# Attention with beacons and an ELU feed-forward layer: w_in in eight wide transfers, v halves by even and odd columns, and a new order of all steps

## The chip, the cores and the metric

The kernel runs on one core of one Trainium2 chip. The metric is the device time of one execution in microseconds (us). Three executions of the kernel before the change took 333.45, 333.01 and 333.42 us, with a median of 333.42 us.

## The reference: what is computed

Eight batches of eight heads, 576 tokens, 64 columns a head, and 16 beacon keys ahead of each head's own keys. The beacons are seen by every query, the own keys causally. The result, laid out as 4608 tokens of 512 numbers, goes through a feed-forward layer.

```python
k_all = np.concatenate([beacon_k, k], axis=2)
v_all = np.concatenate([beacon_v, v], axis=2)
scores = scale * np.matmul(q, k_all.transpose(0, 1, 3, 2))
...
a = np.exp(scores)
a /= a.sum(-1, keepdims=True) + 1e-09
...
x = np.ascontiguousarray(attn_out.transpose(0, 2, 1, 3)).reshape(B * S, H * D)
h = x @ w_in
g = np.where(h > 0.0, h, alpha * (np.exp(np.minimum(h, 0.0)) - 1.0))
return (g @ w_out).astype(np.float32)
```

w_in has 512 rows and 2048 columns, w_out 2048 rows and 512 columns, and the output is 4608 by 512 in float32.

## The kernel before, in words

**Order.** Nothing here is scheduled by a compiler. The program is a list of some 1,550 short words in `run("""...""")`; each word calls one small function ("step") that puts its instructions on their engines. So each engine works through its own instructions in the order of the words, and waits for what they need. A word is a step's letter and its numbers: F.0.1 is the step F for token tile 0, unit 1. Words that matter here:

- lq, lv, wi, wo: the loads, issued on POOL. lq.b.n.h0.h1 loads q and k of batch b (line 136), lv.b.j a piece of 128 keys (the first also holds the 16 beacons, the last has 80) of v (lines 147 and 152), wi a piece of w_in (line 161), wo.i a quarter of w_out (line 165). lk.b.i copies q or k of the batches 3 to 7 into a scratch in DRAM in a type of half the size (line 795), and lt.b.i brings them back transposed by two transfers on SP (line 802). lt.b.0 brings q's and lt.b.1 k's.
- T, ck, cq: transposes of q and k on PE (line 276) for the batches 0 to 2, drained by ACT or DVE (line 289). S is a score matmul (line 330), x its exponential on ACT (line 345), m a causal mask on DVE (line 350).
- L, n: the row sums on PE (line 390, with a column of ones) and their reciprocals on ACT (lines 451 and 454). W is attention times v on PE (line 390 too: one helper, quad, serves both), and M scales it into x, which is stored as xT, features by tokens, on DVE (lines 488, 498, 505). For batch 0 these steps come in two pieces, A (queries 0 to 255) and B (256 to 575), so that the first token tile can begin early.
- F: x times w_in on PE (line 528); e and u: the exponential and the positive part on ACT (lines 538 and 543); k, or r and g: the ELU put together on DVE (lines 553, 560, 566).
- G, o, s: g times w_out for the token tiles 0 and 1, its copy out of PSUM by DVE into a buffer osb (line 582), and the store by SP (line 588). From tile 2 on, w_out is multiplied by a Strassen scheme in seven products: Q on PE (line 650), wt and Z for the sums of its operands (line 596), J for the sums of its results, which for four of the seven end in a buffer osb and a store by SP (lines 671 and 674). From tile 4 on, w_in is partly done so too (H, X, P, K, E, U, V).
- warm, wm, wh: matmuls of zeros that keep PE at work early (lines 206, 214, 223).

**Buffers.** osb has three buffers, shared by o and J: a step that fills one waits until an earlier store from it has landed. A store is queued on SP behind whatever the list puts ahead of it there, the transposing transfers of lt among them. v has two buffers (batches in turn). POOL's loads use eight semaphores in turn, so that a load also waits until the one eight places ahead of it has landed.

**Features.** x's 512 features lie in four chunks of 128 partitions. Four heads share a pair of chunks, each on 32 partitions: the first 32 of a head's 64 columns go to one chunk, the others to the other. Line 390's matmul takes such 32 columns of v as its stationary operand, and w_in's rows are loaded to fit: 32 partitions and two chunks at a time.

Of the kernel before, what the change touches and what calls it, by code (L numbers as in the profile page):

```python
# [12 lines left out]
ALU = mybir.AluOpType  # L13
# [4 lines left out]
def kernel(  # L18
# [240 lines left out]
    @step  # L259
    def wi(c, n):  # L260
        load_wi(c, n)
# [119 lines left out]
    def quad(b, g, qa, qe, t, half, first):  # L381


        v16 = None if half is None else vt[b]
        pcs = [(j, max(a, qa), min(e, qe), c + max(a, qa) - a) for (j, a, e, c) in lays[b]
               if max(a, qa) < min(e, qe)]
        for n, (j, a, e, c) in enumerate(pcs):
            for i in range(4):
                h, p = 4 * g + i, 2 * g + i // 2
                nc.tensor.matmul(  # L390
                    out=t[32 * i:32 * (i + 1), a - qa:e - qa],
                    lhsT=ones[0:kc[j], :] if half is None else v16[0:kc[j], j, h, 32 * half:32 * (half + 1)],
                    rhs=et(b, p)[0:kc[j], i % 2, c:c + e - a],
                    start=(first and n == 0), stop=(n == len(pcs) - 1), skip_group_check=True)
# [206 lines left out]
    def wt(n, h_):  # L601
# [3 lines left out]
        elif n == 2:  # L605
            sub(T2[:, c], B22[:, c], T1[:, c])
        elif n == 3:
            sub(B12[:, c], B22[:, c], B12[:, c])
        else:
            sub(T4[:, c], B21[:, c], T2[:, c])  # L610

    @step
    def Z(t, n, h_, eng="v"):
# [4 lines left out]
        elif n == 1:  # L618
            sub(A(t, h_, 0, 1), A(t, h_, 0, 1), A(t, h_, 1, 1), ALU.add, eng)
        elif n == 2:  # L620
            sub(A(t, h_, 0, 0), A(t, h_, 0, 1), A(t, h_, 0, 0), eng=eng)
        else:
            sub(A(t, h_, 1, 0), A(t, h_, 1, 0), A(t, h_, 0, 0), eng=eng)
# [194 lines left out]
    def run(names):  # L818
        for word in names.split():
            f, *args = word.split(".")  # L820
            op[f](*[a if a in "ABRpvs" else int(a) for a in args])
# [3 lines left out]
    lq.0.0.0.4 warm.12 lq.0.1.0.4 ident bt bk cb.0.3 wm.2 T.0.0.0 T.0.1.0 ck.0.1.0 cb.0.1 cb.0.0  # L825
    cq.0.0.0 cb.0.2 wm.6 S.0.0.0 x.0.0.0 S.0.1.0 x.0.1.0 T.0.0.1 T.0.1.1 ck.0.1.1 cq.0.0.1 wm.6
    S.0.0.3 S.0.0.1 cb.1.0 x.0.0.3 lq.0.0.4.8 T.0.2.0 cq.0.2.0 T.0.3.0 x.0.0.1 S.0.1.2 x.0.1.2 wm.5
    S.0.1.1 x.0.1.1 wm.5 S.0.1.3 x.0.1.3 tri m.0.0.3 m.0.0.0 lq.0.1.4.8 T.0.2.1 cq.0.3.0 S.0.0.2
    x.0.0.2 wm.5 S.0.3.0 T.0.3.1 x.0.3.0 cq.0.2.1 lq.1.0.0.4 S.0.2.0 x.0.2.0 wm.5 S.0.2.1 x.0.2.1
    lv.0.0 lv.0.1 wm.5 S.0.2.3 x.0.2.3 wi.0.0 wi.0.7 lv.0.2 wm.4 T.1.1.0 ck.1.1.0 T.1.0.0 m.0.2.0  # L830
    m.0.1.0 m.0.3.0 L.0.A n.0.A m.0.1.2 m.0.0.2 cq.0.3.1 S.0.3.1 x.0.3.1 cq.1.0.0 W.0.A.0 M.0.A.0
    S.0.3.3 S.0.2.2 x.0.3.3 x.0.2.2 W.0.A.1 m.0.2.3 m.0.3.3 m.0.1.3 M.0.A.1 wh.3 S.0.3.2 wh.5 S.1.2
    x.0.3.2 x.1.2 wh.4 S.1.5 wi.0.5 wi.0.1 x.1.5 wi.0.3 wi.0.6 wi.0.2 wi.0.4 F.0.1 e.0.1 cb.1.1
    S.1.3 x.1.3 F.0.0 u.0.0 e.0.0 lv.0.4 wi.1.0 m.0.3.2 r.0.1 cb.1.2 m.0.2.2 L.0.B lv.0.3 wi.1.3
    W.0.B.0 n.0.B M.0.B.0 g.0.1 S.1.4 F.0.2 x.1.4 S.1.1 e.0.2 x.1.1 k.0.0 W.0.B.1 M.0.B.1 lq.1.0.4.8
    T.1.2.0 ck.1.2.0 r.0.2 g.0.2 F.1.1 u.1.1 e.1.1 T.1.3.0 cq.1.3.0 S.1.6 wi.1.1 cb.1.3 x.1.6 wi.1.7
    wi.1.6 wi.1.5 wi.1.2 wi.1.4 F.0.4 S.1.0 m.1.0.1 wo.0 e.0.4 r.0.4 g.0.4 x.1.0 F.1.7 e.1.7 k.1.1
    r.1.7 g.1.7 S.1.12 x.1.12 S.1.7 cb.2.2 G.0.0.0 x.1.7 F.0.5 e.0.5 r.0.5 S.1.9 x.1.9 g.0.5 F.0.7
    e.0.7 r.0.7 S.1.10 x.1.10 S.1.11 x.1.11 G.0.1.0 F.0.3 g.0.7 m.1.0.0 D.1.0.0 u.0.3 S.1.8 x.1.8
    e.0.3 m.1.1.0 D.1.1.0 k.0.3 F.1.6 u.1.6 cb.2.1 e.1.6 lq.2.0.0.8 T.2.3.0 ck.2.3.0 T.2.2.0  # L840
# [134 lines left out]
```

## Time and profile before

| | us |
|---|---|
| median of three runs | 333.42 |
| the profiled execution itself | 332.93 |
| its span, from first to last instruction | 331.2 |
| PE busy | 321.2 |
| DVE busy | 300.4 |
| ACT busy | 291.8 |
| POOL busy | 100.7 |
| mean granted TensorE clock, share of full speed | 0.994 |

The engines are PE (TensorE matmul), PEld (its weight loads), DVE (VectorE), ACT (ScalarE), POOL (GpSimd) and SP (SyncE). A row of a timeline holds the start, the time taken, engine, line, operation, result<-operands, the shape and the count; behind it, in brackets, stands the idle time of the engine ahead of the row and what ended it. The waits view holds engine, tile and line, what was waited for, and then the total in us, the number of times and the longest. A row of windows holds the stretch, its length, and the busy time (with instructions) of PE, PEld, DVE, ACT and POOL, then the granted clock, the mean busy share of the transfers in flight and GB/s. SPq is SP's own queue. Of a transfer, the row gives the time that its issue takes on the engine; when it lands is told by the line "DMA to landing".

### The profile page before, as it was taken

What the parts mean: (1) busy time and instruction counts of PE and PEld (TensorE: products, weight loads), DVE (VectorE), ACT (ScalarE), POOL (GpSimd) and SP (SyncE); (2) the same over time, 40 slices, a digit from 0 to 9 for tenths busy, and PEclk for the clock granted to TensorE, in tenths of its full rate; (3) what the DMA queues carried; (4) which work ended last, traced back from release to release, by engine and by line L of the source; (5) the groups of instructions that cost most, each with busy time, mean ns of one, the idle gap of its engine ahead of it and who ended that gap; (6) DMA issues with size and microseconds to landing.
All of it is one profiled execution on the core that took longest, in us unless ns stands there. A gap on an engine that the chain in (4) does not pass through costs nothing.

```text
span 331.2 us, 8770 instructions
## 1 busy us (share of the span) xinstructions
PE 321.2 (97%) x3572; PEld 213.8 (65%) x3572; DVE 300.4 (91%) x568; ACT 291.8 (88%) x481; POOL 100.7 (30%) x121
## 2 busy tenths in 40 slices
PE   8989999999999979999999999999999999999995
PEld 3545666544445546765676566756766888888884
DVE  3573999999999799999999999999999999999981
ACT  1989999799999979999999999999988778889941
POOL 8866745583049218900120348000000000000000
PEclk9998999999999999999999999999999999999999
DMA  9999999999989959999591995610111011020113
GB/s 115 141 165 186 204 196 174 163 154 175 65 90 133 147 138 87 193 170 165 75 148 53 119 71 109 91 35 2 63 36 34 0 65 64 2 97 33 34 65 127
DMA packets 129080, 34.65 MB, mean 105 GB/s; under 512 B 112912, under 2 KB 127504, under 8 KB 129040
## 3 DMA queue, kind: packets, MB, share of 16 engines
q0 software_dynamic: 94912, 18.49, 67.5%
q1 hardware_dynamic: 33552, 15.47, 21.3%
q8 instruction: 28, 0.46, 0.6%
q10 hardware_dynamic: 576, 0.13, 0.2%
q14 instruction: 12, 0.10, 0.1%
HBM read 37.22 MB, written 15.34 MB: 159 GB/s over the span
## 4 chain that ended last, share of the span: by engine, by line
PE 78%; DVE 7%; DMA 5%; ACT 4%; POOL 4%; SPq 1%; issue 1%; DVEq 0%; ACTq 0%; POOLq 0%
PE ops L650 25%; PE hps L528 20%; PE hps L732 11%; PE sc L330 6%; PE ut L390 5%; PE ops L575 4%; DMA v<-in_v_dram 3%; DMA out_dram<-osb 2%; PE ut L650 2%; DVE gt L553 1%; SPq L802 1%; DVE qk L410 1%; PE lt L436 1%; POOL qst L136 1%; POOL kst L136 1%
## 5 line engine op out<-in xcount | busy, mean ns | idle before, releaser
L345 ACT ACTIVATE et<-sc 128x1024 f16<-128x1024 f32 (+2 forms) x114 | 105.3, 988 | 3.3 <-PE sc L330 2.9
L528 PE MATMUL hps<-xT,w_in 128*128 128x512 f16 (+1 forms) x448 | 95.4, 350 | 1.7 <-ACT r L543 1.5
L650 PEld LDWEIGHTS <-gt 128*128 128x128 f16 x768 | 74.1, 98 | 16.3 <-issue 2.7
L528 PEld LDWEIGHTS <-w_in 128*128 128x128 f16 x448 | 40.9, 98 | 36.7 <-issue 6.2
L538 ACT ACTIVATE e<-hps 128x512 f32<-128x512 f32 x96 | 59.0, 626 | 3.2 <-DVE gt L553 2.0
L553 DVE SCALAR_TENSOR_TENSOR gt<-e,r 128x512 f16<-128x512 f32 x84 | 56.5, 681 | 0.0
L543 ACT ACTIVATE r<-hps 128x512 f16<-128x512 f32 x84 | 51.5, 622 | 3.1 <-PE hps L528 2.6
L147 POOL DMA_DIRECT2D v<-in_v_dram x40 | 44.1, 1192 | 26.4 <-PE ut L390 13.5
L650 PE MATMUL ops<-w_out,gt 128*128 128x256 f16 x368 | 48.4, 273 | 0.0
L650 PE MATMUL ops<-wt,gt 128*128 128x256 f16 x352 | 46.3, 273 | 0.2 <-DVE osb L671 0.2
L596 DVE TENSOR_TENSOR gt<-gt 128x1024 f16<-128x1024 f16 x48 | 32.3, 681 | 0.1
L771 DVE SCALAR_TENSOR_TENSOR gt<-e,r 128x512 f16<-128x512 f32 x48 | 31.8, 681 | 0.1
L350 DVE TENSOR_TENSOR et<-et,triu 128x1024 f16<-128x1024 f16 (+4 forms) x66 | 26.8, 447 | 2.5 <-ACT et L345 2.4
L742 ACT COPY kst<-hps 128x512 f32<-128x512 f32 x36 | 21.3, 594 | 5.6 <-PE hps L732 5.3
L390 PEld LDWEIGHTS <-v 128*32 128x32 f16 (+1 forms) x800 | 17.6, 96 | 12.0 <-issue 2.6
L390 PE MATMUL ut<-et,v 128*32 128x464 f16 (+3 forms) x560 | 21.1, 296 | 0.4 <-ACT et L345 0.4
L732 PEld LDWEIGHTS <-w_in 128*128 128x128 f16 x192 | 18.6, 98 | 2.9
L671 DVE TENSOR_TENSOR osb<-ops,sm 128x512 f32<-128x512 f32 x23 | 15.6, 683 | 3.6 <-DMA out_dram<-osb 2.3
L810 POOL MEMSET qst<- 128x96 bf16 x5 | 0.9, 178 | 55.8 <-PE sc L330 53.3
L410 DVE TENSOR_TENSOR qk<-qk,et 128x1344 f16<-128x1344 f16 (+2 forms) x30 | 17.5, 582 | 0.2
L488 DVE TENSOR_TENSOR xT<-ut,rl 128x672 f16<-128x672 f32 (+12 forms) x26 | 16.4, 668 | 0.2
L575 PE MATMUL ops<-w_out,gt 128*128 128x512 f16 x64 | 16.2, 381 | 0.0
(126 smaller groups left out, 524.6 us busy)
## 6 DMA issues: line engine op xcount, KB each, us to landing
out_dram<-osb SPq DMA_DIRECT2D x35, 256.0 KB, 2.3
v<-in_v_dram POOLq DMA_DIRECT2D x24, 128.0 KB, 8.1
scr<-in_q_dram POOLq DMA_DIRECT2D x5, 576.0 KB, 9.2
scr<-in_k_dram POOLq DMA_DIRECT2D x5, 576.0 KB, 13.9
w_in<-in_moe_w_in_dram POOLq DMA_DIRECT2D x16, 128.0 KB, 6.7
w_out<-in_moe_w_out_dram POOLq DMA_DIRECT2D x4, 512.0 KB, 10.8
v<-in_v_dram POOLq DMA_DIRECT2D x8, 112.0 KB, 6.2
v<-in_v_dram POOLq DMA_DIRECT2D x8, 80.0 KB, 5.8
```

What stands on the lines that cost most here:

```text
L147: nc.gpsimd.dma_start(out=vt[b][r0:r0 + n, j, :, :], in_=v[b, :, ilo[j]:ilo[j] + n, :].rearrange("h s d -> s h d"),)
L345: nc.scalar.activation(out=ets[b, d][:, :, a - EC2 * d:e - EC2 * d], in_=sc[b, g][:, :, a - c0:e - c0], func=AFT.Exp, bias=0.0, scale=SCALE)
L390: nc.tensor.matmul(out=t[32 * i:32 * (i + 1), a - qa:e - qa], lhsT=ones[0:kc[j], :] if half is None else v16[0:kc[j], j, h, 32 * half:32 * ...
L528: nc.tensor.matmul(out=h[:, n_, :], lhsT=w_in16[:, cc, P * fc:P * (fc + 1)], rhs=xt[k][:, cc, a - TT * k:e - TT * k], start=(cc == 0), sto ...
L538: nc.scalar.activation(out=eb[t, i], in_=flat(hp[t, i]), func=AFT.Exp, bias=0.0, scale=1.0)
L543: nc.scalar.activation(out=rb[t, i], in_=flat(hp[t, i]), func=AFT.Relu, bias=0.0, scale=1.0)
L553: nc.vector.scalar_tensor_tensor(out=half(t, i), in0=eb[t, i], scalar=1.0, in1=rb[t, i], op0=ALU.subtract, op1=ALU.min)
L575: nc.tensor.matmul(out=ob[t, tb_], lhsT=gt[:, fc, P * tb_:P * (tb_ + 1)], rhs=w_out16[:, fc, :], start=(fc == 0), stop=(fc == NFC - 1))
L596: (nc.vector if eng == "v" else nc.gpsimd).tensor_tensor(out=o_, in0=a_, in1=b_, op=op_)
L650: nc.tensor.matmul(out=xy[t, n_][qd], lhsT=lw[:, P * qd:P * (qd + 1)], rhs=wt_[:, c, :], start=(first and c == 0 and (qd == 0 or (t, n_) n ...
L732: nc.tensor.matmul(out=hx[t, g, n_][:, c, :], lhsT=lw, rhs=rh, start=(first and c == 0 and k_ == 0), stop=(k_ == 1), skip_group_check=True)
L771: eng.scalar_tensor_tensor(out=o_, in0=v_(eb[t, g, ph]), scalar=1.0, in1=v_(rb[t, g, ph]), op0=ALU.subtract, op1=ALU.min)
```

## The change

1. w_in comes in 8 transfers of 128 partitions by 2 by 512 columns (256 KB each) instead of 16 of 32 partitions by 2 by 1024 columns (128 KB each). The feature that a partition holds changes with it: a pair of chunks g holds the features 256 g + 2 p + t, t naming the chunk. So half t of a head's v is now every second column, and line 390 takes its stationary operand with a step of two.
2. Two operand sums change their sign and so do those that go with them: wt.2 and Z.2 are turned around, wt.4 adds. Z gets a variant "d" by a transfer, which the new list never calls.
3. The list of words is a new one from its first line to its last. It has the same compute steps; the zero matmuls differ by 2 of 3,572 PE instructions.

```diff
-    wi_v = moe_w_in.rearrange("(g i t d) f -> i d g t f", i=4, t=2, d=32)
+    wi_v = moe_w_in.rearrange("(g p t) f -> p g t f", p=P, t=2)
...
-    def load_wi(c, n):
-        f_ = slice(DF // 2 * c, DF // 2 * (c + 1))
-        g, i = n // 4, n % 4
-        nc.gpsimd.dma_start(
-            out=w_in16[32 * i:32 * (i + 1), 2 * g:2 * g + 2, f_], in_=wi_v[i, :, g, :, f_])
+    def load_wi(f0, f1, g):
+        f_ = slice(P * f0, P * f1)
+        nc.gpsimd.dma_start(out=w_in16[:, 2 * g:2 * g + 2, f_], in_=wi_v[:, g, :, f_])
...
-                    lhsT=ones[0:kc[j], :] if half is None else v16[0:kc[j], j, h, 32 * half:32 * (half + 1)],
+                    lhsT=ones[0:kc[j], :] if half is None else v16[0:kc[j], j, h, half:D:2],
...
-            sub(T2[:, c], B22[:, c], T1[:, c])
+            sub(T2[:, c], T1[:, c], B22[:, c])
...
-            sub(T4[:, c], B21[:, c], T2[:, c])
+            sub(T4[:, c], B21[:, c], T2[:, c], ALU.add)
...
-    lv.0.0 lv.0.1 wm.5 S.0.2.3 x.0.2.3 wi.0.0 wi.0.7 lv.0.2 wm.4 T.1.1.0 ck.1.1.0 T.1.0.0 m.0.2.0
+    wm.3 S.0.3.2 x.0.3.2 m.0.2.3 m.0.3.2 n.0.A wm.4 T.1.0.0 cq.1.0.0 T.1.1.0 lv.0.1 wi.0.4.1 W.0.A.1
```

What the new list moves is read from the order of each engine's instructions. **POOL, the first loads.** In the rows, v is piece by piece: the row of 112 partitions is lv.b.0, that of 80 is lv.b.4. qst_89 and kst_90 hold batch 1. Before, behind the loads of batch 0's first heads and the mask:

```order
L136 DMA qst_87<-in_q_dram 80x4x256
L136 DMA kst_88<-in_k_dram 80x4x256
L136 DMA qst_89<-in_q_dram 96x4x384
L136 DMA kst_90<-in_k_dram 96x4x384
L147 DMA v_363<-in_v_dram 112x8x64
L152 DMA v_363<-in_beacon_v_dram 16x8x64
L147 DMA v_363<-in_v_dram 128x8x64
L161 DMA w_in_81<-in_moe_w_in_dram 32x2x1024 x2
L147 DMA v_363<-in_v_dram 128x8x64
L161 DMA w_in_81<-in_moe_w_in_dram 32x2x1024 x6
L147 DMA v_363<-in_v_dram 80x8x64
L161 DMA w_in_81<-in_moe_w_in_dram 32x2x1024
```

And of the change, from the same place:

```order
L136 DMA kst_88<-in_k_dram 80x4x256
L147 DMA v_300<-in_v_dram 128x8x64
L246 MEMSET triu 128x384
L248 AFFINE_SELECT triu<-triu 128x128
L248 AFFINE_SELECT triu<-triu 128x256
L147 DMA v_300<-in_v_dram 80x8x64
L136 DMA qst_89<-in_q_dram 96x4x384
L136 DMA kst_90<-in_k_dram 96x4x384
L147 DMA v_300<-in_v_dram 112x8x64
L152 DMA v_300<-in_beacon_v_dram 16x8x64
L147 DMA v_300<-in_v_dram 128x8x64
L160 DMA w_in_81<-in_moe_w_in_dram 128x2x512 x3
```

Two pieces of v (lv.0.2 and lv.0.4) now stand ahead of batch 1's q and k, and lv.0.0 and lv.0.1 behind them follow each other as before. The A steps of batch 0 read the pieces 0, 1 and 2; before, piece 2 stood behind two transfers of w_in, and now no piece that they read stands behind any. **ACT, the same stretch**, where line 345 (343 in the change) is an exponential of scores, and line 289 (287) drains a transpose. Before:

```order
L345 ACTIVATE et<-sc 128x2x416 x10
L289 COPY qk_104<-tp 128x2x576
L451 ACTIVATE rl<-la 128x512
L454 ACTIVATE rl<-rl 128x512
L345 ACTIVATE et<-sc 128x2x416 x4
L345 ACTIVATE et<-sc 128x2x512 x2
L538 ACTIVATE e<-hps 128x512
```

And of the change:

```order
L343 ACTIVATE et<-sc 128x2x416 x13
L449 ACTIVATE rl<-la 128x512
L452 ACTIVATE rl<-rl 128x512
L287 COPY qk_104<-tp 128x2x576
L343 ACTIVATE et<-sc 128x2x416
L343 ACTIVATE et<-sc 128x2x512
L343 ACTIVATE et<-sc 128x2x416
L536 ACTIVATE e<-hps 128x512
```

The row sums' reciprocals (n.0.A) stand behind three more exponentials and ahead of the drain. **SP, where batch 4 is brought in.** scr_1702 and scr_1977 are batch 4's scratch before (scr_1631 and scr_1627 in the change); the store of osb_2002 is s.1.1, that of osb_2217 J.2.1. Before:

```order
L802 DMA_TRANSPOSE qst1_89<-scr_1702 128x2x576
L802 DMA_TRANSPOSE qst1_89<-scr_1977 128x2x576
L802 DMA_TRANSPOSE kst1_90<-scr_1702 128x2x576
L802 DMA_TRANSPOSE kst1_90<-scr_1977 128x2x576
L588 DMA out_0_dram<-osb_2002 128x512
L674 DMA out_0_dram<-osb_2217 128x2x256
```

And of the change, where osb_1942 is s.1.0 and osb_1824 s.1.1:

```order
L802 DMA_TRANSPOSE qst1_89<-scr_1631 128x2x576
L802 DMA_TRANSPOSE qst1_89<-scr_1627 128x2x576
L586 DMA out_0_dram<-osb_1942 128x512
L802 DMA_TRANSPOSE kst1_90<-scr_1631 128x2x576
L802 DMA_TRANSPOSE kst1_90<-scr_1627 128x2x576
L586 DMA out_0_dram<-osb_1824 128x512
L674 DMA out_0_dram<-osb_2217 128x2x256
```

The buffer that J.2.1 fills was last held by s.1.1 before and is last held by s.1.0 now; s.1.0 has moved ahead of the two transposing transfers. Further on, SP in the change goes on so (osb_2592 is J.2.5, osb_2616 J.2.6, osb_2811 J.3.1, osb_1461 s.0.0; scr_2082 is batch 5's k):

```order
L802 DMA_TRANSPOSE kst1_90<-scr_2068 128x2x576
L802 DMA_TRANSPOSE kst1_90<-scr_2082 128x2x576
L674 DMA out_0_dram<-osb_2592 128x2x256
L674 DMA out_0_dram<-osb_2616 128x2x256
L802 DMA_TRANSPOSE qst1_89<-scr_2557 128x2x576
L802 DMA_TRANSPOSE qst1_89<-scr_2084 128x2x576
L674 DMA out_0_dram<-osb_2811 128x2x256
L674 DMA out_0_dram<-osb_3108 128x2x256
L802 DMA_TRANSPOSE kst1_90<-scr_2557 128x2x576
L802 DMA_TRANSPOSE kst1_90<-scr_2084 128x2x576
L674 DMA out_0_dram<-osb_3126 128x2x256
L674 DMA out_0_dram<-osb_3180 128x2x256
```

In the list before, the stores of J.2.4 and J.2.5 both stand ahead of batch 5's k, and s.0.0 stands near the front of SP's order. Now J.2.5's store stands behind batch 5's k, and s.0.0 is the next row after those shown: until then its buffer of the three is not free.

More of the change, by code (lines that the diff above doesn't have):

```diff
@@ L259, in wi @@
     @step
-    def wi(c, n):
-        load_wi(c, n)
+    def wi(f0, f1, g):
+        load_wi(f0, f1, g)
     @step
@@ L617, in Z @@
             sub(s3[:, c], A(t, h_, 0, 0), A(t, h_, 0, 1), eng=eng)
-        elif n == 1:
-            sub(A(t, h_, 0, 1), A(t, h_, 0, 1), A(t, h_, 1, 1), ALU.add, eng)
         elif n == 2:
-            sub(A(t, h_, 0, 0), A(t, h_, 0, 1), A(t, h_, 0, 0), eng=eng)
+            sub(A(t, h_, 0, 0), A(t, h_, 0, 0), A(t, h_, 0, 1), eng=eng)
         else:
-            sub(A(t, h_, 1, 0), A(t, h_, 1, 0), A(t, h_, 0, 0), eng=eng)
+            o_, i_ = (A(t, h_, 0, 1), A(t, h_, 1, 1)) if n == 1 else (A(t, h_, 1, 0), A(t, h_, 0, 0))
+            if eng == "d":
+                nc.gpsimd.dma_start(out=o_, in_=i_, accum_op=ALU.add)
+            else:
+                sub(o_, o_, i_, ALU.add, eng)
     xy, sm = {}, {}
@@ L820, in run @@
             f, *args = word.split(".")
-            op[f](*[a if a in "ABRpvs" else int(a) for a in args])
+            op[f](*[a if a in "ABRpvsd" else int(a) for a in args])
     run("""
[L825 to L828, printed above, removed]
@@ new lines @@
+    X.6.4 e.5.10 Q.4.49.56 Q.4.56.63 F.5.14 u.5.10 k.5.10 x.6.11 Z.4.4.1 Z.4.4.0 U.5.0.5 u.5.14
+    S.6.8 e.5.14 S.6.12 x.6.12 F.5.7 Q.4.63.70 J.4.3 e.5.7 x.6.8 lt.7.1 m.6.1.0 V.5.0.5 k.5.14
+    Q.4.70.77 F.5.15 D.6.0.1 D.6.0.2 D.6.0.3 Q.4.77.84 X.6.3 Z.5.3.1 u.5.15 lv.7.1 lv.7.4 lv.7.2
+    lv.7.3 lp.7.1 u.5.7 k.5.7 lp.7.0 S.7.4 S.7.3 e.5.15 k.5.15 F.6.9 E.5.0.4 V.5.0.4 x.7.3 J.4.4
+    x.7.4 u.6.9 e.6.9 F.6.12 e.6.12 Q.4.84.91 Q.4.91.98 u.6.12 Z.5.1.1 S.7.1 L.6.0 P.6.0.0
+    Q.4.98.105 K.6.0.0 J.4.5 Z.5.3.0 Z.5.1.0 D.6.1.0 P.6.0.1 K.6.0.1 n.6.0 M.6.0.0 Q.4.105.112
@@ new lines @@
+    K.9.1.1 Q.8.14.21 U.9.0.5.v Z.8.1.0 P.9.1.3 K.9.1.2 P.9.1.4 E.9.0.5 V.9.0.5 K.9.1.3 Q.8.21.28
+    P.9.1.5 E.9.1.1 K.9.1.4 J.8.0 U.9.1.1 P.9.1.6 U.9.1.6 Z.8.2.0 Q.8.28.35 Z.8.2.1 E.9.1.6 V.9.0.6
+    Q.8.35.42 P.9.2.0 K.9.1.5 J.8.1 Q.8.42.49 U.9.1.4 E.9.1.4 P.9.2.1 V.9.1.1 V.9.1.6 K.9.2.0
+    K.9.2.1 J.8.2 Z.8.4.0 U.9.1.5 P.9.2.2 K.9.2.2 Q.8.49.56 P.9.2.3 E.9.1.5 V.9.1.5 P.9.2.4
+    Q.8.56.63 K.9.2.3 P.9.2.5 U.9.2.1 E.9.2.1 K.9.2.4 U.9.2.4 V.9.1.4 K.9.2.5 E.9.2.4 V.9.2.1
+    V.9.2.4 P.9.2.6 E.9.2.6 Q.8.63.70 U.9.2.6 P.9.3.0 K.9.3.0 J.8.3 Q.8.70.77 Z.9.3.0 P.9.3.1
@@ new lines @@
+    K.9.3.1 P.9.3.2 E.9.2.5 K.9.3.2 Q.8.77.84 Z.8.4.1 P.9.3.3 P.9.3.4 Q.8.84.91 U.9.2.5 K.9.3.3
+    P.9.3.5 V.9.2.6 J.8.4 Q.8.91.98 K.9.3.4 Q.8.98.105 V.9.2.5 E.9.3.1 U.9.3.1 U.9.3.4 K.9.3.5
+    Q.8.105.112 V.9.3.1 E.9.3.4 U.9.3.5 V.9.3.4 P.9.3.6 E.9.3.5 Z.9.1.0 V.9.3.5 Z.9.3.1 J.8.6
+    U.9.3.6 Q.9.0.8 Q.9.8.16 E.9.3.6 V.9.3.6 Z.9.2.0 Q.9.16.24 J.9.0 Z.9.1.1 Q.9.24.32 Z.9.2.1
+    Q.9.32.40 Q.9.40.48 J.9.2 J.9.1 Q.9.48.56 Q.9.56.64 J.8.5 Z.9.4.1 Z.9.4.0 J.9.3 Q.9.64.72
+    Q.9.72.80 J.9.4 Q.9.80.88 Q.9.88.96 J.9.5 Q.9.96.104 Jh.9.0 Q.9.104.112 Jh.9.1
```

219 lines of the change are left out of this document (103 added, 116 removed).

## The prediction

> **What bounds the kernel now.** I read the page's totals first, then windows by stage, then the waits and the timelines of the two stages where PE stands still.
>
> ```profile
> span 331.2 us, 8770 instructions
> PE 321.2 (97%) x3572; PEld 213.8 (65%) x3572; DVE 300.4 (91%) x568; ACT 291.8 (88%) x481; POOL 100.7 (30%) x121
> PEclk9998999999999999999999999999999999999999
> ```
>
> PE is busy for 321.2 of 331.2 us, so PE's 10.0 idle us and its clock are all that an order can win. The new list has the same compute and about 0.05 us less of zero matmuls. The windows tell where the idle time lies (after the length: busy PE, PEld, DVE, ACT, POOL, clock):
>
> ```profile
> 0.00:20.00 20.00, 17.70 (x264) 9.66 (x266) 10.12 (x36) 12.80 (x17) 14.68 (x28) 1.00 1.22 137
> 20.00:60.00 40.00, 37.91 (x624) 24.64 (x624) 31.36 (x59) 36.92 (x53) 24.23 (x35) 0.96 1.52 184
> 60.00:100.00 40.00, 39.96 (x388) 18.30 (x386) 38.98 (x74) 38.14 (x61) 17.59 (x18) 1.00 1.55 126
> 100.00:140.00 40.00, 37.95 (x397) 23.70 (x396) 37.22 (x72) 37.53 (x60) 25.15 (x21) 1.00 1.42 142
> 140.00:300.00 160.00, 159.99 (x1655) 113.04 (x1654) 159.68 (x295) 147.14 (x256) 19.04 (x24) 1.00 0.54 73
> 300.00:331.20 31.20, 27.73 (x254) 24.44 (x251) 23.06 (x39) 19.25 (x39) 0.00 (x0) 0.99 0.20 69
> ```
>
> Idle PE is 2.3 us at the start, 2.1 in 20 to 60, nothing to speak of in 60 to 100 and 140 to 300, 2.05 in 100 to 140, and 3.5 at the end (the last copy and store). Start and end keep their form. So two places can pay: 20 to 60, where the clock also falls, and 100 to 140.
>
> **First place: v and the clock, 20 to 30 us.**
>
> ```profile
> 22.13 0.39 PE L390 MATMUL ua<-et,v 128*32 128x16 f16 x16 [1.41 <-DMA v<-in_v_dram]
> ...
> 26.51 1.31 PE L528 MATMUL hps<-xT,w_in 128*128 128x256 f16 x8
> ...
> 29.05 1.25 PE L390 MATMUL lt<-et,ones 128*32 128x320 f16 x40
> ```
>
> PE waits 1.41 us for piece 2 of v. Then, by windows of the length for which the clock is down:
>
> ```profile
> 20.25:23.66 3.41, 2.00 (x60) 1.20 (x59) 1.79 (x4) 2.51 (x5) 3.33 (x6) 1.00 1.08 170
> 23.66:27.07 3.41, 3.39 (x23) 1.30 (x23) 1.79 (x8) 3.04 (x5) 3.41 (x7) 0.50 1.40 138
> ```
>
> Half speed for 3.41 us, with PE busy for 3.39 of it, costs 1.70 us of PE work. Wait and clock together are 3.1 us: the most that this place can give. What it does give is set by ACT, which must reach the reciprocals of batch 0's second piece (n.0.B):
>
> ```profile
> 10.95 7.70 ACT L345 ACTIVATE et<-sc 128x832 f16<-128x832 f32 x10
> ...
> 22.85 2.38 ACT L345 ACTIVATE et<-sc 128x832 f16<-128x832 f32 x3 [0.86 <-PE sc L330]
> 25.54 2.10 ACT L345 ACTIVATE et<-sc 128x1024 f16<-128x1024 f32 x2 [0.32 <-PE sc L330]
> 27.85 0.60 ACT L538 ACTIVATE e<-hps 128x512 f32<-128x512 f32 x1 [0.21 <-PE hps L528]
> ...
> 30.36 0.70 ACT L451 ACTIVATE rl<-lt 128x640 f32<-128x640 f32 x1
> ```
>
> Between 10.95 and 30.36 ACT is idle for 0.86 + 0.32 + 0.21 = 1.39 us. In the new order it has the same exponentials and copies ahead of n.0.B (16 of the narrow form and 3 of the wide), but only one e instead of two: 0.60 less. With no idle time, n.0.B would start at 30.36 - 1.39 - 0.60 = 28.4. So **the first term is -2.0 us**, of the possible 3.1.
>
> Does v come in time? POOL's issues, and times to landing:
>
> ```profile
> 11.51 0.93 POOL L147 DMA_DIRECT2D v<-in_v_dram  x1
> v<-in_v_dram POOLq DMA_DIRECT2D x1, 128.0 KB, 8.9
> 13.47 8.61 DMA v<-in_v_dram
> w_in<-in_moe_w_in_dram POOLq DMA_DIRECT2D x1, 128.0 KB, 4.6
> kst<-in_k_dram POOLq DMA_DIRECT2D x1, 288.0 KB, 7.1
> ```
>
> Piece 1 landed at 11.51 + 8.9 = 20.4, piece 2 at 13.47 + 8.61 = 22.1, with two w_in between: three times 128 KB in 1.7 us, 0.55 each. The eighth w_in landed at 27.1 (issued 22.48, 4.6), six w_in and 80 KB of v behind piece 2: 5.0 us for 848 KB, 0.75 per 128 KB. In the new order the pieces 2 and 4 (208 KB) go ahead and piece 1 is last: 20.4 plus 208 KB at 0.55 to 0.75, so 21.3 to 21.6. PE asked for piece 2 at 22.13 - 1.41 = 20.7; in the new order one exponential or two more pace it there, so up to about 0.7 us of waiting stays, partly covered by ACT's queue.
>
> **w_in.** The first unit of F now needs two transfers (512 KB) behind piece 1, not eight: 21.5 plus 2.2 to 3.0, so 23.7 to 24.6, where before it began at 26.51 and its last transfer landed at 27.1. That moves an e earlier on ACT, which may idle 0.3 to 0.5 us for it. Up to batch 1's second q and k the same 1,280 KB of w_in stand ahead, so those land at 32.2 (25.14 + 7.1, the k of that pair) as now. Their transposes:
>
> ```profile
> 34.39 0.63 PE tp L276 x24
> ```
>
> That leaves 2.1 us for a lead of 2.0: enough, but only just. A new transfer has 1,024-byte runs to each of 128 partitions, a form of w_in that this trace doesn't show. Its nearest row is w_out, in four transfers with the same runs, whose landing is set by the queue. I take the service of 0.55 to 0.75 per 128 KB for both forms; at the higher end every w_in would be 0.2 per 128 KB later, 0.8 us on the four that matter first, and I keep that in the range. Eight issues less on POOL (0.54 each) hide behind its waits for semaphores.
>
> **Columns of v in steps of two.** The weight loads of v took 96 ns for 32 columns, those of w_in 98 for 128, so time isn't in what they read, and PEld is busy for 65%:
>
> ```profile
> L528 PEld LDWEIGHTS <-w_in 128*128 128x128 f16 x448 | 40.9, 98 | 36.7 <-issue 6.2
> L390 PEld LDWEIGHTS <-v 128*32 128x32 f16 (+1 forms) x800 | 17.6, 96 | 12.0 <-issue 2.6
> ```
>
> I take 0; if each of 800 took 4 ns more in the open, it would be 3 us, but 17.6 busy us lie under running matmuls. The changed signs have the shapes that they had: 0.
>
> **Second place: a store behind the transposing transfers, 100 to 140 us.**
>
> ```profile
> 101.55 5.88 SPq L802 DMA_TRANSPOSE kst<-scr  x2
> 103.37 4.06 SPq L802
> 107.49 7.57 DMA out_dram<-osb
> 115.18 0.69 DVE osb L671
> 121.67 1.02 PE L528 MATMUL hps<-xT,w_in 128*128 128x512 f16 x4 [1.50 <-ACT r L543]
> ...
> 123.57 1.51 PE L390 MATMUL ut<-et,v 128*32 128x464 f16 x40 [0.39 <-ACT et L345]
> DVE osb L671 <- DMA out_dram<-osb: 2.3, 1, 2.3
> ```
>
> J.2.1 needs an osb buffer whose store s.1.1 stands on SP behind batch 4's k. The store is issued at 107.49, lands at 115.06, and DVE waits 2.3 us; PE pays 1.50 + 0.39 = 1.9 us later. Now J.2.1 takes the buffer of s.1.0, which goes out ahead of those two transfers (5.88 us of issue, from 101.55 on). Even with the longest landing that a store shows between 100 and 150 us, 7.6 (its row stands below), it is down by 109.2, and J.2.1 is wanted at 115.18 - 2.31 = 112.9. So **the second term is -1.9**. What is late next there is s.1.1, for a J two places on.
>
> **Sum.** -2.0 - 1.9 = -3.9. Against it I set +0.6: half of the 0.7 for piece 1, and half of the 0.3 to 0.5 for the first e. The profiled execution took 332.93, so 329.6; the median of the runs shown is 0.49 above that: **330.1 us**.
>
> **The rivals.**
>
> *The clock still falls.* The drop came after a window with 2.00 us of busy PE, yet this one, a whole number of such windows later, was busy for less and the clock held:
>
> ```profile
> 119.24:122.65 3.41, 1.91 (x8) 1.00 0.57 115
> 122.65:126.06 3.41, 3.02 (x62) 1.00 0.76 215
> ```
>
> So idle time alone doesn't decide it; the early window held narrow matmuls (32 columns), the later one full ones. The new order is paced by ACT there too, with the same narrow matmuls, and may idle as long in smaller pieces. Price: the 1.70 again, 331.8. Chance 0.22, a late piece 1 included. The Trainium skill, "TensorE: Matmul & The Clock Gate", section "What's actually happening", has the clock fall after an idle window of about 3.4 us. The length agrees with the 3.41 us here; the condition doesn't, as the trace's drop followed only 1.41 us of waiting. By that rule nothing in the new order could bring the drop, and this rival would have no chance.
>
> *The store wait moves* to another J, so that only the first term is left: 330.1 + 1.9 = 332.0. Chance 0.09. *The new list doesn't do what it says*, both waits come back elsewhere: 333.4, chance 0.05.
>
> *Slower: J.2.5's store.* It now stands behind batch 5's k on SP, and s.0.0 keeps one osb buffer out of use, so that J.3.1 must wait for it.
>
> ```profile
> 134.89 6.73 SPq L802 DMA_TRANSPOSE kst<-scr  x2
> 146.39 0.67 DVE L671 TENSOR_TENSOR osb<-ops,sm 128x512 f32<-128x512 f32 x1
> L802 SPq DMA_TRANSPOSE kst<-scr x10: 1295/2502/4445, 71.9 to 201.8; - x10
> DMA to landing us min/median/max: 2.2/5.3/7.6
> ```
>
> J.3.1 ran at 146.4. Batch 5's k were through at 134.89 + 6.73 = 141.6; a store behind them lands at 143.8, 146.9 or 149.2 by the shortest, median and longest landing of a store between 100 and 150 us. At the median that is 0.5 us late, which PE can mostly absorb. With two issues of 4.45 instead, 8.9, and the longest landing it lands at 151.4, 5.0 late, and PE would lose some 4.5 (it lost 1.9 of 2.3 before): 330.1 + 4.5 = 334.6. It decides from about 3.5 us late on, where the whole gain is gone. Chance 0.19, which also holds its like: a new list may queue another store or load so.
>
> **How the numbers follow.** The forecast has 0.45, the rivals 0.22, 0.09, 0.05 and 0.19. Low end: both upper bounds, 3.1 + 2.3 = 5.4 below 333.42, so 328.0. High end: 334.2, most of the way to the slow rival, which leaves out less than 2 in 10; the 0.8 of w_in lies within. A measurement can tell 0.2%, 0.67 us, from no change: faster means below 332.75, slower above 334.09. Faster: 0.44 + 0.18 + 0.05 = 0.67; same: 0.01 + 0.04 + 0.04 + 0.03 + 0.02 = 0.14; slower: 0.02 + 0.17 = 0.19.
>
> **What would show it.** Right: no wait of line 390 for v, no half-clock window past the start, n.0.B at about 28.4, F's first at 24 to 25; no wait of DVE's osb for a store in 100 to 140; PE busy without a gap from 140 on, and a span of about 328. Wrong: the waits view names osb or w_in with over 1 us, POOL's loads idle long on semaphores, or PE has gaps in 60 to 300 that it didn't have.

## The result and the profile after

The changed kernel takes 328.88 us (328.86 to 328.95, 4 runs) against 333.29 us before (333.01 to 333.45, 4 runs): a ratio of 0.9869, 95% interval 0.9852 to 0.9886, so 4.4 us faster. The forecast was 330.1 us and the range 328.0 to 334.2: the kernel became faster, as forecast, and came out 1.2 us below the forecast. The profiled execution took 328.88 us, like the median.

The page of the change first:

```profile
span 327.2 us, 8741 instructions
PE 318.9 (97%) x3566; PEld 214.0 (65%) x3570; DVE 300.2 (92%) x568; ACT 290.5 (89%) x481; POOL 92.0 (28%) x113
...
PEclk9999999999999999999999999999999999999999
```

PE is busy for 2.3 us less (321.2 before), most of which is the half-speed stretch that is gone, and idle for 8.3 us instead of 10.0. The same windows as before show where:

```profile
0.00:20.00 20.00, 16.80 (x241) 9.14 (x246) 9.41 (x33) 12.88 (x17) 17.28 (x31) 1.00 1.31 147
20.00:60.00 40.00, 38.57 (x696) 26.67 (x693) 34.25 (x69) 37.63 (x55) 18.84 (x23) 1.00 1.48 180
60.00:100.00 40.00, 39.91 (x362) 18.38 (x359) 38.77 (x68) 38.41 (x61) 18.11 (x23) 1.00 1.66 131
100.00:140.00 40.00, 39.95 (x416) 25.33 (x415) 39.80 (x77) 39.72 (x64) 22.02 (x19) 1.00 1.83 156
140.00:300.00 160.00, 160.00 (x1652) 113.58 (x1650) 159.03 (x293) 146.54 (x258) 15.79 (x21) 1.00 0.42 69
300.00:327.20 27.20, 23.67 (x217) 20.90 (x215) 18.97 (x32) 15.30 (x31) 0.00 (x0) 0.99 0.21 71
```

100 to 140 us has lost its gap (0.05 us idle, 2.05 before), and the clock of 20 to 60 is 1.00 instead of 0.96. The early stage, on PE and then on ACT:

```profile
20.97 0.96 PE L388 MATMUL ua<-et,v 128*32 128x256 f16 x48
...
23.55 1.05 PE L526 MATMUL hps<-xT,w_in 128*128 128x256 f16 x8
...
26.34 1.25 PE L388 MATMUL lt<-et,ones 128*32 128x320 f16 x40
```

```profile
10.32 9.96 ACT L343 ACTIVATE et<-sc 128x832 f16<-128x832 f32 x13
...
24.75 0.62 ACT L536 ACTIVATE e<-hps 128x512 f32<-128x512 f32 x1
25.22 1.98 ACT L343 ACTIVATE et<-sc 128x1024 f16<-128x1024 f32 x2
27.03 0.66 ACT L541 ACTIVATE r<-hps 128x512 f16<-128x512 f32 x1
27.64 0.70 ACT L449 ACTIVATE rl<-lt 128x640 f32<-128x640 f32 x1
```

All 48 matmuls of W for batch 0's first piece run in one row with no wait for v, the first F starts at 23.55 (26.51 before), and ACT, without a bracket from 10.32 on, reaches n.0.B at 27.64 (30.36 before). Of that lead of 2.7 us, 2.1 are left at L.1.1 (54.2 after, 56.3 before) and 1.8 at L.3.0 (105.3 and 107.2). The rest of the 4.0 us at the end comes behind that.

### The profile page after: what moved, and what is told of

Read it like the earlier page. It is cut to its first block, busy times and chain, and to the rows that moved or that the text cites. A ratio compares the mean times of both kernels' runs of the same rounds, so it can differ in the third digit from the quotient of the medians.

```text
span 327.2 us, 8741 instructions
## 1 busy us (share of the span) xinstructions
PE 318.9 (97%) x3566; PEld 214.0 (65%) x3570; DVE 300.2 (92%) x568; ACT 290.5 (89%) x481; POOL 92.0 (28%) x113
## 4 chain that ended last, share of the span: by engine, by line
PE 80%; ACT 14%; DVE 2%; issue 1%; DMA 1%; ACTq 0%; DVEq 0%
PE ops L650 27%; PE hps L526 22%; PE hps L732 11%; ACT et L343 8%; PE sc L328 6%; PE ut L388 6%; PE ops L573 3%; PE ut L650 2%; ACT r L541 2%; ACT e L536 2%; PE lt L434 1%; DMA lo<-in_beacon_k_dram 1%; ACT qk L287 1%; DVE gt L564 1%; DVE r L558 1%
## 5 line engine op out<-in xcount | busy, mean ns | idle before, releaser
L541 ACT ACTIVATE r<-hps 128x512 f16<-128x512 f32 x84 | 53.0, 635 | 2.2 <-PE hps L526 1.9
L147 POOL DMA_DIRECT2D v<-in_v_dram x40 | 39.2, 1013 | 39.1 <-PE ut L388 23.1
L348 DVE TENSOR_TENSOR et<-et,triu 128x1024 f16<-128x1024 f16 (+5 forms) x66 | 26.9, 448 | 1.9 <-ACT et L343 1.8
L650 PE MATMUL ops<-w_out,s 128*128 128x256 f16 x112 | 15.0, 273 | 0.0
```

The lines of the kernel that those rows point to most:

```text
L147: nc.gpsimd.dma_start(out=vt[b][r0:r0 + n, j, :, :], in_=v[b, :, ilo[j]:ilo[j] + n, :].rearrange("h s d -> s h d"),)
L348: nc.vector.tensor_tensor(out=o, in0=o, in1=i, op=ALU.mult)
L541: nc.scalar.activation(out=rb[t, i], in_=flat(hp[t, i]), func=AFT.Relu, bias=0.0, scale=1.0)
L650: nc.tensor.matmul(out=xy[t, n_][qd], lhsT=lw[:, P * qd:P * (qd + 1)], rhs=wt_[:, c, :], start=(first and c == 0 and (qd == 0 or (t, n_) n ...
```

## The experiments

All times of "before" in this part are from the same chip as the run that they stand beside. There the kernel before had medians of 332.8, 332.5 and 332.2 us (35, 23 and 16 runs), and single executions from 331.4 to 335.3. So its 333.3 beside the result is nearer to its slower executions. Three variants of the change below, which gain and lose next to nothing (328.94, 328.97 and 329.09 us), are 3.1 to 3.6 us faster than the kernel before on their own chip, not 4.4.

**The store, moved alone (b_store).**

```diff
-lk.5.1 lt.4.1 s.1.1 Q.2.7.14
+lk.5.1 s.1.1 lt.4.1 Q.2.7.14
```

> The kernel before with one word moved: s.1.1 stands ahead of lt.4.1 on SP, nothing else. Theory: the wait of J.2.1 for that store is a term of its own, worth the 1.9 us that PE stood still behind it. Then DVE's osb no longer waits for a store between 100 and 140 us, PE's idle time there falls from 2.05 us to under 0.2, and the time is 331.4 us (331.1 to 331.8). Rival: the two transfers of batch 4's k, now 0.6 us later, or the next store become the wait, and what is won is given back: 332.8 to 333.4, with a new row of over 1 us in the waits.

Measured: 331.11 us against 332.8, ratio 0.9956 (0.9938 to 0.9974). DVE's wait is gone, but PE has a new one (PE's timeline, then the waits):

```profile
115.33 0.39 PE L330 MATMUL sc<-kst 64*128 64x272 bf16 x4 [1.63 <-DMA kst<-scr]
```

```profile
PEld L330 <- DMA kst<-scr: 2.1, 1, 2.1
```

SP issued batch 4's two transfers behind the store, and PE waited 1.63 us for that k. By starts of steps in the two profiles, the stretch from L.3.0 to J.3.0 shrank from 37.4 to 36.6 us: 0.8, not 1.9. The rest of the gain between the two profiles is the early stage, which the edit doesn't touch: this one has no half-speed stretch, and its n.0.B stands at 29.23 instead of 30.36. Among the executions of both kernels with a mean clock above 0.995, the medians differ by 1.2 us (331.07 and 332.24). The rival had the mechanism right, though it gave back only part.

**v earlier, alone (b_v), and the wait filled (b_fill).**

```diff
-lv.0.0 lv.0.1 wm.5 S.0.2.3 x.0.2.3 wi.0.0 wi.0.7 lv.0.2 wm.4
+lv.0.0 lv.0.1 lv.0.2 wm.5 S.0.2.3 x.0.2.3 wi.0.0 wi.0.7 wm.4
```

> The kernel before with one word moved: lv.0.2 stands directly behind lv.0.1, ahead of two transfers of w_in instead of behind them. Piece 2 should land about 1.0 us earlier (21.0 instead of 22.1), so PE's wait of 1.41 us falls to some 0.4. Theory one (the clock falls because of the idle time of that window): the window then has 1 us more of busy PE, no half-speed stretch follows, and the time is 331.5 to 332.3. Theory two (the narrow matmuls of that window decide, the wait only adds): the half-speed stretch of 3.41 us stays, and the time is 332.6 to 333.3.

```diff
-cq.1.0.0 W.0.A.0 M.0.A.0
+cq.1.0.0 wh.24 W.0.A.0 M.0.A.0
```

> The kernel before with six matmuls of zeros (512 columns each, about 1.3 us) put ahead of W.0.A.0, so that PE is at work while it waits for piece 2 of v, which lands as before (22.1). Theory one (the clock follows how much PE works, zeros too, and the wait is its cause): no half-speed stretch from 23.7 to 27.1, the 1.70 us of PE work that it cost are free, and the time is 331.7 to 332.4, since ACT then sets the pace. Theory two (the drop isn't caused by that wait): a stretch of 3.41 us at 0.50 stays, and the time is 333.1 to 333.6. The difference to the run with piece 2 moved is the price of the wait by itself.

Measured: 332.38 us (ratio 0.9991, 0.9968 to 1.0014) and 332.13 us (0.9989, 0.9968 to 1.0010): neither can be told from no change. Yet in both profiles the clock holds, and b_v has no wait for v left. The clock holds in b_store's profile as well, where v stands in its old place and PE waits 0.54 us for it, and in 2 of b_v's 12 executions and 1 of b_fill's the mean clock is still 0.995 or less. So neither run shows that the wait brings the drop. PE's timeline of b_v shows what was next:

```profile
22.12 0.56 PE L390 MATMUL ua<-et,v 128*32 128x256 f16 x24
...
25.36 0.38 PE L528 MATMUL hps<-xT,w_in 128*128 128x256 f16 x2 [0.75 <-PE sc L330]
26.07 0.81 PE L528 MATMUL hps<-xT,w_in 128*128 128x256 f16 x6 [0.34 <-DMA w_in<-in_moe_w_in_dram]
27.15 1.05 PE L528 MATMUL hps<-xT,w_in 128*128 128x256 f16 x8
```

The first F stops after two of its eight matmuls and waits 0.34 us for w_in. ACT waits for that F in turn: 0.95 us in this profile. n.0.B comes at 29.43, no earlier than the 29.23 of b_store: where the clock holds, taking the wait for v away gained nothing here, as w_in stood behind it. In b_fill's profile the zeros fill PE's time instead: its first F starts at 25.45 without a wait, and n.0.B comes at 29.08.

**All three (b_three).** The edits of b_store, b_v and b_fill together.

> The kernel before with all three: s.1.1 ahead of lt.4.1, lv.0.2 directly behind lv.0.1, and six matmuls of zeros ahead of W.0.A.0. Theory (two terms that add, neither of which needs the rest of the new order): -1.9 and -1.2 to -1.7, so 329.7 to 330.2 against 333.3 before and 328.9 of the change. Rival (the early term needs the new order of ACT or w_in by column quarters): only the store's term shows, 331.2 to 331.6.

Measured: 331.34 us, ratio 0.9960 (0.9932 to 0.9988), the store's share as in b_store. PE waits 1.79 us for batch 4's k. The theory of two terms that need nothing else fell: the late one isn't whole without k in time, and the early one doesn't come from v's wait.

**Part 1 alone (b_wide), undone (a_w16).** The new `wi_v`, `load_wi` and `half:D:2` in the old list, and the old ones in the new list, with the words for the transfers at their places:

```diff
-wi.0.0 wi.0.7 lv.0.2
+wi.0.4.0 lv.0.2
...
-wi.0.5 wi.0.1 x.1.5 wi.0.3 wi.0.6 wi.0.2 wi.0.4 F.0.1
+wi.0.4.1 x.1.5 wi.4.8.0 wi.4.8.1 F.0.1
```

> The kernel before with part 1 of the change alone: w_in in 8 transfers of 128 partitions by column quarters at the places of the 16, and the halves of v by even and odd columns; the old order of everything else. Theory (the transfers' form by itself costs and gives nothing, since the queue serves bytes): the wait for piece 2 of v and the half-speed stretch stay, piece 2 now stands behind one transfer of 256 KB, and the time is 333.1 to 333.5. The weight loads of v take 96 ns as before. Rival one (a transfer of 128 partitions is served faster): w_in's first half lands over 1 us earlier than 27.1 and the time falls to 332.5 or below. Rival two (columns in steps of two cost PE): 800 weight loads of v with a few ns more each, 333.8 to 336.

```diff
-lv.0.1 wi.0.4.1 W.0.A.1 M.0.A.1 cb.1.1 W.0.A.0 wi.0.4.0 M.0.A.0 wi.4.8.1 lv.0.3
+lv.0.1 wi.0.4 wi.0.5 W.0.A.1 M.0.A.1 cb.1.1 W.0.A.0 wi.0.0 wi.0.1 M.0.A.0 wi.0.6 wi.0.7 wi.0.2 wi.0.3 lv.0.3
```

> The changed kernel with part 1 undone: w_in in 16 transfers of 32 partitions by column halves and the halves of v in blocks of 32 columns, the new order otherwise. F.0.0 then needs 1 MB behind piece 1 of v instead of 512 KB. Theory (column quarters are what lets F begin before ACT asks for it): that megabyte lands at about 24.5 to 25, F.0.0 starts 1.0 to 1.5 us later than 23.55, ACT's queue and DVE's H.1.0 stand behind it, and the time is 329.7 to 330.5 against 328.9. Rival (the form of the transfers doesn't matter and the order alone does it): 328.7 to 329.2.

Measured: part 1 alone 331.20 us against 332.49, ratio 0.9963 (0.9949 to 0.9978), with all 12 runs between 330.98 and 331.52. Part 1 undone in the new list: 331.96 us (330.31 to 332.94), 3.1 us more than the change and more than the 329.7 to 330.5 of its theory. My theory for b_wide, that the transfers by themselves give nothing, is wrong. PE's timeline of b_wide:

```profile
20.79 0.39 PE L388 MATMUL ua<-et,v 128*32 128x16 f16 x16 [0.30 <-DMA v<-in_v_dram]
...
24.69 1.05 PE L526 MATMUL hps<-xT,w_in 128*128 128x256 f16 x8
26.00 1.05 PE L526 MATMUL hps<-xT,w_in 128*128 128x256 f16 x8
26.98 1.25 PE L388 MATMUL lt<-et,ones 128*32 128x320 f16 x40
```

F runs through at 24.69, and L.0.B starts at 26.98: 2.1 us earlier than in the profile before, 0.9 earlier than in b_store's (27.92), and 0.6 later than in the change. At L.1.1 it stands at 54.3, nearly like the change (54.2); b_store stands at 55.1. POOL's issues show one thing that part 1 moves, first in the kernel before, then in b_wide:

```profile
12.42 1.09 POOL L161 DMA_DIRECT2D w_in<-in_moe_w_in_dram  x2
15.93 0.55 POOL L161 DMA_DIRECT2D w_in<-in_moe_w_in_dram  x1 [1.51 <-DMA qst<-in_q_dram]
18.39 0.54 POOL L161 DMA_DIRECT2D w_in<-in_moe_w_in_dram  x1 [1.92 <-DMA kst<-in_k_dram]
19.57 2.21 POOL L161 DMA_DIRECT2D w_in<-in_moe_w_in_dram  x4 [0.64 <-DMA v<-in_v_dram]
22.48 0.54 POOL L161 DMA_DIRECT2D w_in<-in_moe_w_in_dram  x1
```

```profile
12.22 0.70 POOL L160 DMA_DIRECT2D w_in<-in_moe_w_in_dram  x1
13.82 0.70 POOL L160 DMA_DIRECT2D w_in<-in_moe_w_in_dram  x1
```

The first F reads the first eight transfers of the kernel before, and six of them are issued only from 15.93 on, behind POOL's waits for earlier loads (the eight semaphores that are used in turn). It reads two of b_wide's, and both are issued ahead of the first such wait. So part 1 makes the first F need fewer bytes and fewer issues at once; no run here takes these two apart. And with part 1 undone, F waits in the new order too:

```profile
25.31 1.05 PE L528 MATMUL hps<-xT,w_in 128*128 128x256 f16 x8 [1.45 <-DMA w_in<-in_moe_w_in_dram]
```

In 7 of its 12 executions the mean clock was 0.995 or less (332.4 us in the median of those, 330.8 of the others).

**The wide form by halves (b_half).** The new feature order and 128 partitions, but 4 transfers of 512 KB by column halves.

```diff
-wi.0.0 wi.0.7 lv.0.2
+lv.0.2
...
-wi.0.5 wi.0.1 x.1.5 wi.0.3 wi.0.6 wi.0.2 wi.0.4 F.0.1
+wi.0.8.0 x.1.5 wi.0.8.1 F.0.1
```

> The kernel before with w_in in 4 transfers of 128 partitions by column halves (512 KB each; v halves by even and odd columns): the wide form without the split by quarters, the old order otherwise, and no transfer of w_in ahead of piece 2 of v. F.0.1 then needs a whole megabyte, as before, where with quarters it needs 512 KB. Theory one (the split by columns is what counts: fewer bytes ahead of the first F): F.0.1 starts at 25.5 to 27, n.0.B at 28.9 to 30, and the time is 331.8 to 332.6 at full clock, no better than before. Theory two (the form, 128 partitions, is what counts): n.0.B at 28.3 to 28.6 and 331.0 to 331.4, as with quarters. A spread of the runs of under 0.6 us would put the spread of before (331.4 to 335.3) down to the transfers of 32 partitions.

Measured: 331.72 us, ratio 0.9982 (0.9966 to 0.9998), from 331.07 to 332.99. Between the two: its profiled execution (331.13) has n.0.B at 28.36, as theory two wants, with a first F that needs a whole megabyte and starts at 24.72 without a wait. But the runs scatter over 1.9 us, against 0.5 with quarters on another chip. So the gain is smaller and less sure than with quarters, and the bytes alone don't explain it: both transfers that this F reads were issued by 14.6 us, as few and as early as in b_wide. Whether that counts, or the form, or only that no transfer of w_in stands ahead of piece 2 of v here, this run doesn't tell apart.

**The store by another buffer (b_s10), and with part 1 (b_wide_s10).** s.1.0 goes out behind batch 4's q and ahead of its k, as in the new list, and s.1.1 stays where it was.

```diff
-lk.4.1 lt.4.0 Q.2.0.7
+lk.4.1 lt.4.0 s.1.0 Q.2.0.7
...
-lt.5.0 s.1.0 e.3.9
+lt.5.0 e.3.9
```

> The kernel before with the one word s.1.0 moved directly behind lt.4.0, nothing else. Theory (the store's term is 1.9 us where batch 4's k isn't held up): PE's idle time in 100 to 140 us falls from 2.05 to under 0.4, and the profiled span is shorter by 1.9 than one of before with the same start of n.0.B, so 330.0 to 330.6 in the median if w_in's landing scatters as it did. Rival (k of batch 4 takes the place of the store): 331.2 to 331.9 and a wait of PE for it of over 1 us.

> The kernel before with part 1 (w_in in 8 transfers by column quarters, v halves by even and odd columns) and one word moved: s.1.0 stands directly behind lt.4.0 on SP, where SP is idle, so that J.2.1's buffer is free early and batch 4's k is held up by no store. Theory (the whole change comes from w_in's column quarters and from this store, not from the rest of the new list): 331.2 of part 1 alone, less 1.9 of the wait, so 329.3 us (329.0 to 329.7), against 328.9 of the change; no wait of osb and none of PE for batch 4's k over 0.5 us. Rival (batch 4's k is the next bound in the old order, as where s.1.1 was moved ahead of it: PE waited 1.63 us for it): 330.3 to 330.9.

Measured: 329.37 us (328.66 to 332.22, ratio 0.9919, 0.9887 to 0.9951) for the one word, and 329.11 us (328.80 to 329.15, ratio 0.9898, 0.9878 to 0.9917) with part 1. The one word gained 2.9 us in the median, more than its theory's 1.9, but over six executions that lie 3.6 us apart: the interval allows 1.6 to 3.8. Beside it, part 1 adds only 0.3 us, less than these runs can tell, where alone it gave 1.3; what part 1 does show there is the narrow spread. b_s10's profile is of its slowest execution, with a lower clock. Its span is only 0.8 us shorter than that of the profile before, with L.0.B at the same place (29.01 and 29.05). PE has no gap in 100 to 140 us there, as the theory wants, but waits 1.71 us for w_out at 41.77, which the profile before doesn't have. The windows of PE alone for 100 to 140 us, b_wide first, then b_wide_s10:

```profile
100.00:140.00 40.00, 37.90 (x394) 1.00 1.41 142
```

```profile
100.00:140.00 40.00, 40.00 (x418) 1.00 1.58 146
```

In b_wide_s10, PE has no gap left, and no wait for batch 4's k. So two edits in the old list give 329.1 us, where the whole new list gives 328.9.

**Zeros taken out of the change (a_bare).**

```diff
-x.0.3.3 wm.3 S.0.3.2
+x.0.3.3 S.0.3.2
...
-n.0.A wm.4 T.1.0.0
+n.0.A T.1.0.0
...
-ck.1.1.0 wh.3 S.1.5 x.0.3.1 x.1.5 wh.4 S.0.2.1
+ck.1.1.0 S.1.5 x.0.3.1 x.1.5 S.0.2.1
```

> The changed kernel without the four groups of zero matmuls between 18 and 23.5 us (wm.3, wm.4, wh.3, wh.4; about 0.8 us of PE at full speed), the order otherwise as it is. PE then stands still for 0.8 us more there, without any wait added. Theory one (the clock follows a window's work, and the early windows with their narrow matmuls lie near the limit): a half-speed stretch of 3.41 us appears between 20 and 30 us, and the time is 329.8 to 330.7. Theory two (a wait of over 1 us at one place is needed): the clock holds, and since ACT sets the pace there, the time stays at 328.7 to 329.1.

Measured: 328.94 us (328.83 to 329.04), and none of the six executions has a lower clock (0.998 or more). That much less work of PE doesn't bring the drop back.

**ACT's first exponentials (a_swap, a_lead).**

```diff
-cb.0.1 T.0.0.0 T.0.1.0 ck.0.1.0
+cb.0.1 T.0.1.0 T.0.0.0 ck.0.1.0
```

> The changed kernel with two words swapped: T.0.1.0 ahead of T.0.0.0, so that the transposes that the first exponential waits for run first and don't wait for the second use of a bank. In the profile of the change ACT then works without a gap from the first exponential at 8.99 us to n.0.B at 27.64, and that stretch is on the chain of waits. Theory (ACT's start sets the early stage): the first exponential starts at about 8.4, n.0.B and all behind it come 0.4 to 0.6 us earlier, and the time is 328.3 to 328.5. Rival (loads or the second exponential's scores take it back): 328.8 to 329.1.

```diff
-bk cb.0.2 cb.0.1 T.0.0.0 T.0.1.0 ck.0.1.0 cq.0.0.0 cb.0.3 cb.0.0 wm.8 S.0.1.0 x.0.1.0 S.0.0.0 T.0.1.1 ck.0.1.1 T.0.0.1 x.0.0.0 wm.5
+bk cb.0.1 cb.0.0 T.0.1.0 T.0.0.0 ck.0.1.0 cq.0.0.0 cb.0.2 cb.0.3 S.0.1.0 x.0.1.0 S.0.0.0 x.0.0.0 wm.8 T.0.1.1 ck.0.1.1 T.0.0.1 wm.5
```

> The changed kernel with its first words in another order: cb.0.1 and cb.0.0 ahead of the other two, T.0.1.0 first, and both first score matmuls and exponentials ahead of the zero matmuls and of ck.0.1.1. In the run with only the two T swapped, ck.0.1.0 came 0.46 us earlier, but the first exponential only 0.1, as two zero matmuls stood ahead of its scores, and ACT then idled again ahead of ck.0.1.1. Theory (ACT's first microseconds set the early stage): the first exponential at 8.4 to 8.6, n.0.B 0.2 to 0.4 us earlier than 27.64, 328.5 to 328.7. Rival (the landing of the early loads or the later F take it back): 328.8 to 329.0.

Measured: 328.97 and 329.09 us: no gain. ACT's timeline of a_lead:

```profile
8.41 1.62 ACT L343 ACTIVATE et<-sc 128x832 f16<-128x832 f32 x2 [0.46 <-PE sc L328]
10.09 0.69 ACT L287 COPY qk<-tq 128x640 bf16<-128x640 bf16 x1
11.22 1.62 ACT L343 ACTIVATE et<-sc 128x832 f16<-128x832 f32 x2 [0.44 <-PE sc L328]
```

The first exponential comes 0.6 us earlier, as wanted, but the third waits for the scores behind ck.0.1.1's drain, and by 11.2 the lead is gone.

## Why the prediction came out as it did

**First term, -2.0 by ACT's chain: near in size, in part by luck, and wrong in its cause.** n.0.B came at 27.64 (28.4 forecast; where the 0.8 us more came from is open), and 2.1 us of lead were left at L.1.1. But the step that named the wait for v and the clock as what the new order gains here was wrong. b_v and b_fill, whose profiles show neither, gained nothing that can be measured; b_wide left v's order as it was and stands at L.1.1 like the change. Of the 2.1 us there, 1.1 lie between the profile before and b_store's, which has the same early words and no half-speed stretch: they belong to the one execution that was profiled. Another 0.8 lie between b_store and b_wide, so by these single profiles they come with w_in's new form, and 0.1 is left for the rest of the new order. In the medians that form alone gave 1.3 us, and beside b_s10 only 0.3, within that run's scatter: its price is less sure than its place.

My working had rows for w_in and misread one. The transfer that was issued at 22.48 and landed at 27.1 is the ninth, which the first F doesn't read. The eighth is the last in the row of four from 19.57 on: issued at about 21.2, it landed at about 25.8 by my estimate, taking the ninth's 4.6 us. That is 0.7 us ahead of F at 26.51. So in that execution w_in stood close behind the wait for v, and the half speed held F longer, so that no row showed PE waiting for it. I read w_in only as a condition that the new order must meet, not as what would be late next. The 0.75 us per 128 KB that I took from the wrong row would be 0.62 (six transfers in 3.7 us), so the high end of that working was too high.

The forecast gain was 3.3 us. The variants of the change on their own chips put it at 3.1 to 3.6, and the 4.4 beside the result stands on executions of the kernel before that took longer than its medians elsewhere. That the 3.3 comes so near is luck in part: the first term counted 1.1 us of one execution's state, and the allowance took 0.6 off for waits that didn't come.

**The clock.** In the kernel before, 15 of 74 executions beside the experiments had a mean clock of 0.995 or less, like the profile before with its 0.994, and among the 35 beside b_store these took 333.7 us in the median, the others 332.2. So the 1.70 is about the right price, 1.5 by those runs, but of an event in one execution of five, which the profile before happened to show. None of the 40 executions of kernels with the quarters had it, a_bare's among them, but 7 of 12 of a_w16 did. The Trainium skill, "TensorE: Matmul & The Clock Gate", section "What's actually happening", calls the window free-running, so that one program falls into it differently from execution to execution; the 15 of 74 agree with that. The profiles don't agree with its condition of a whole idle window: the clock fell with 1.41 us of waiting in the profile before and with 1.58 in that of b_s10, and held with 1.45 in that of a_w16. What decides it was not settled.

**Second term, -1.9: right.** PE's idle time in 100 to 140 us fell by 2.0 in the profiles. b_wide and b_wide_s10 give 2.1 us between their medians, on two chips; b_s10 by itself gave 2.9, with an interval that holds 1.9. The mechanism is as put, J.2.1 takes a buffer whose store went out ahead of batch 4's k. "What is late next there is s.1.1" was not the whole of it: had s.1.1 been moved instead, k itself would have been next, as b_store shows.

**The allowance of +0.6** was for waits that didn't come. Piece 1 of v caused none, and ACT had no gap ahead of the first e. **The 0.49** between the profiled execution and the median before was scatter of the kernel before, not something that the change would inherit. These two are most of the 1.2 us.

**The slow rival** had its mechanism, but not its price. SP's timeline of the change, the landing of the first of those two stores, and DVE's timeline:

```profile
130.77 6.22 SPq L802 DMA_TRANSPOSE kst<-scr  x2
137.04 1.10 SPq L674 DMA_DIRECT2D out_dram<-osb  x2
```

```profile
out_dram<-osb SPq DMA_DIRECT2D x1, 256.0 KB, 7.4
```

```profile
145.84 0.68 DVE L671 TENSOR_TENSOR osb<-ops,sm 128x512 f32<-128x512 f32 x1
```

The store of J.2.5 was issued at 137.04 behind batch 5's k and took 7.4 us to land, so it was down at 144.4. J.3.1 ran at 145.84 without waiting: 1.4 us to spare. Batch 5's k was issued 4 us earlier than before, which is what the two leads together allowed. The rival in which the store wait moves to another J didn't come either. The waits view does name osb once, with 3.8 us of ACT, but that is at 322.83, where ACT stood idle for the same 3.78 us before and the wait was put down to PE.

**Columns of v in steps of two**: 0, as taken.

```profile
L388 PEld LDWEIGHTS <-v 128*32 128x32 f16 (+1 forms) x800 | 17.8, 96 | 9.7 <-issue 2.1
```

## What to carry to other kernels

Ask of each wait that a change removes what would end last without it, and look for it also where a slower clock hides it: here the first weights, a megabyte in eight transfers, stood close behind a visible wait of 1.4 us. Of the edits to the early stage alone, loading them in quarters by the columns that the first use needs gave 1.3 us; loading them in halves gave a gain barely clear of nothing, and the two edits to the visible wait gave none that can be measured. Where two things on one queue are both wanted soon, moving one ahead of the other trades waits; freeing the buffer by a third transfer, when the queue is idle, doesn't. Before pricing a stage from one profile, look at how far the executions of that kernel lie apart.

## What the runs showed of the hardware

The landing of the first loads scatters between profiles of kernels that issue them alike: batch 1's first k, issued at 9.3 to 9.5 us in the kernels with the old list, landed between 16.9 and 18.1 us. In groups of six executions or more, the kernels whose first F needs a megabyte lie 1.6 to 4.2 us apart from fastest to slowest, executions with a lower clock included; those whose first F needs half of it keep within 0.6 us. That the landing is what parts them is likely but not shown, as each kernel left one trace only.
